# Block-sparse attention and a mixture of experts: weight splits with further buffers and in V's memory, transfers behind k's transposition, and score matmuls over 128 partitions

## The chip, the cores and the metric

The kernel runs on one core of one Trainium2 chip. The metric is the time of one execution on the device in microseconds (us); the kernel before takes 2201.07 us, the median of three runs (2196.04 to 2204.06). Its profile shows one further execution. The engines are called as the profile calls them: PE (TensorE, matmuls), PEld (PE's weight loads), DVE (VectorE), ACT (ScalarE), POOL (GpSimd) and SP (SyncE, which here issues all DMAs).

## The reference

Attention with a block mask comes first. Its output is the input x of a layer with eight experts, all of which are computed for every row and weighted by a matrix P that alternating row and column normalisation makes from x's logits.

```python
scores = 1.0 / np.sqrt(D) * np.matmul(q, k.transpose(0, 1, 3, 2))   # B, H, S, D = 4, 8, 768, 64
scores = np.where(mask, scores, -1e9)      # blocks of 32: window, first, last, 3 random ones
attn = softmax(scores)
x = (attn @ v).transpose(0, 2, 1, 3).reshape(B * S, H * D)          # 3072 x 512
logits = x @ w_gate
P = np.exp(logits - logits.max())
for _ in range(8):
    P /= P.sum(1, keepdims=True) + 1e-09
    P /= P.sum(0, keepdims=True) + 1e-09
    P *= N / E
for e in range(8):
    out += P[:, e:e + 1] * (np.maximum(x @ w1[e], 0.0) @ w2[e])      # 512 -> 1024 -> 512
```

## The kernel before

**Numbers as pairs.** Inputs are float32, matmuls take float16. A float32 operand is therefore split into a high and a low float16 part, and a product is three matmuls into one accumulator: high by high, high by low, low by high. A weight quadrant is split by an ACT instruction for the high part (`first_high` L275, `queue_split` L1184) and one or two DVE instructions for the low part (`first_low` L278, L1191).

**Attention.** 32 pairs of batch and head ("heads", n = 0 to 31) of six column tiles each make 192 steps T. A step has score matmuls twice: `m` (L689, L692), whose row maximum DVE takes (`top`, L698), and `t` (L722, L725), with the maximum subtracted through extra rows, whose exponential ACT takes (`pe`, L730). The first matmul of each covers 128 rows; the second one adds the low part of q and the masks' rows and covers only the rows in use, `ROWS_M` = 88 or `ROWS_T` = 98 (L443). `split_lo` (L740 to L744) finishes the weights, `values` (L787) multiplies by V three steps later, and L806 to L825 normalise and write x. Heads are handled two at a time, so a pair has 12 steps. `turn` (L675) turns q (16 steps ahead) and k (14 steps ahead, phase 4 of 6) by DMA; the scores of the pair begin 10 steps ahead of its weights. `lower` (L702) fills in rows that belong to the maxima and turns q's second part again (L710).

**The order.** A planner fixes the place of every instruction in attention. Fixed pieces stand at a step and a class (`at`); chains of optional jobs (weight loads, their sums, their splits) are dealt into steps by `deal()`, from planned microseconds of DVE, ACT and POOL for each. Each engine then runs its instructions in that order. SP runs in order too, and waits with an instruction until its source is ready.

**The passage from one to the other.** As soon as a batch's x is there, `x_split` and `x_store` (L303 to L313) split its column blocks for the expert layer and store them (384 KB each) in `xd`; `load_x1` (L247) loads the first tiles back. Expert 0's `w1` is loaded, scaled by its maximum, summed and split during attention. Its `w2` is loaded and scaled there and has four of its eight sums made; all of its seven splits come after attention. Of batch 3, the last steps of x (`finish_x` L373) run `LATE` = 34 product slots into the expert layer.

**The expert layer.** A stage i = 4e + b is expert e on batch b. Both matrix products go by a scheme of seven products on quadrants. `stage1` (L1315) has four column parts qi; in each the products p = 0, 1, 5, 6, 3, 4, 2 come as six groups of three matmuls of 128x384, land in four PSUM banks, and are combined by DVE (`comb`, L1336), ACT (L1371) and POOL; a column part takes about 13.8 us. `stage2` (L1435) makes the products `py` in the order 1, 0, 5, 6, 3, 4, 2 and adds them into `acc` (L1464 to L1480). One expert takes about 221 us. Products of stage i + 1 alternate with outputs of stage i. Beside them a queue of side work (`Slots`, L1109) runs weight splits when the planned time of the engine allows it, or when a product needs them (`need`).

**The weights of the next expert.** `w1` has one set of seven float16 buffers (`w1p`, in the arena and the attic, L236 to L245). In the last column part of an expert's last batch, each product p, once issued, frees its buffer, and `split_w1` (L1216) queues the split of the next expert's quadrant into it (L1324, `used[p]()`). All seven splits thus lie between the first products of that column part and the first ones of the next expert. `w2` has seven buffers of 4 KB (`w2p`, L1076), refilled during the next expert's stages by `split_w2` (L1239).

## Time and profile before

| quantity | value |
|---|---|
| median of three runs | 2201.07 us |
| profiled execution | 2201.64 us |
| its span | 2199.9 us, 1.74 us less than its time |
| PE, share of the span busy | 98% |
| DVE | 78% |
| POOL | 65% |
| ACT | 58% |
| attention | the first 415 us |
| one expert | about 221 us |
| granted TensorE clock, mean | 0.998 |

A group row of the profile names line, engine, operation, output and inputs, shape and count, then the busy time in us with the mean of one instruction in ns, and after a second bar the time for which the engine stood idle just before such instructions, with what ended that time. A timeline row has the start and the duration in us, then the same names, and in brackets the idle time before it. A window row has its bounds, its length, and for each engine the busy time and the number of instructions in it; at its end the granted clock, the share of the DMA engines and their GB/s.

### The profile page before, as it was taken

To read this page: it belongs to the slowest core of one execution; us is meant where nothing else is said; L and a number is where in the kernel's file an instruction comes from. 1 tells how busy PE (TensorE), PEld (TensorE's weight loads), DVE (VectorE), ACT (ScalarE), POOL (GpSimd) and SP (SyncE) were. 2 spreads that over 40 slices of the span, in tenths; PEclk is the share of its full clock that TensorE was granted. 3 is DMA by queue.
4 is the path that set the end of the run, shared out by engine and by line. 5 is a ranking of instruction groups with operands and counts; after the bars stand their busy time and mean duration, and the time that the engine had idled before them with its cause. 6 is when DMAs were issued, how large, how long until landed. Compare 5 with 4: busy or idle time off the path is not lost.

```text
span 2199.9 us, 47055 instructions
## 1 busy us (share of the span) xinstructions
PE 2150.8 (98%) x18796; PEld 1591.8 (72%) x18796; DVE 1706.8 (78%) x2970; ACT 1282.8 (58%) x2385; POOL 1432.6 (65%) x1476
## 2 busy tenths in 40 slices
PE   6999999999999999999999999999999999999999
PEld 4777676667777777777777777777777777777777
DVE  8889889677878767876887688768876887688765
ACT  5888888666466546554655465546554655465442
POOL 4667768477568656765676567656765686567553
PEclk9999999999999999999999999999999999999999
DMA  6757796122121212121212121212121212131221
GB/s 170 180 130 171 171 198 146 42 100 84 58 89 51 90 51 90 51 90 51 89 52 89 51 89 51 89 51 89 51 89 51 90 51 89 51 90 58 80 80 51
DMA packets 195632, 192.34 MB, mean 87 GB/s; under 512 B 132412, under 2 KB 150868, under 8 KB 195412
## 3 DMA queue, kind: packets, MB, share of 16 engines
q1 hardware_dynamic: 194848, 189.30, 30.6%
q8 instruction: 147, 2.41, 0.4%
q14 instruction: 73, 0.60, 0.1%
q10 hardware_dynamic: 564, 0.03, 0.0%
HBM read 140.54 MB, written 17.30 MB: 72 GB/s over the span
## 4 chain that ended last, share of the span: by engine, by line
PE 72%; DVE 11%; POOL 7%; ACT 4%; issue 4%; DMA 1%; POOLq 0%; DVEq 0%; ACTq 0%
PE py L1456 31%; PE p L1324 30%; PE u L787 3%; PE m L689 2%; PE t L722 2%; PE m L692 2%; PE t L725 2%; POOL h L1356 2%; DVE top L698 1%; ACT h L1345 1%; POOL s L1404 1%; DMA kt<-ks 1%; POOL r L1202 1%; DVE h L1356 1%; DVE attic L1191 1%
## 5 line engine op out<-in xcount | busy, mean ns | idle before, releaser
L1456 PE MATMUL py<-w2p,h 128*128 128x256 f16 x8064 | 973.2, 273 | 6.3 <-DVE acc L1480 2.6
L1456 PEld LDWEIGHTS <-h 128*128 128x128 f16 x8064 | 788.9, 98 | 159.0 <-issue 7.4
L1356 POOL TENSOR_TENSOR h<-u,h 128x384 f16<-128x384 f32 x128 | 126.4, 988 | 534.8 <-ACT h L1345 534.8
L1324 PE MATMUL p<-attic 128*128 128x384 f16 x2304 | 421.4, 326 | 3.9 <-DVE attic L1191 2.1
L1324 PEld LDWEIGHTS <-attic 128*128 128x128 f16 x3072 | 299.2, 98 | 173.1 <-DVE attic L1191 6.6
L1324 PE MATMUL p<-arena 128*128 128x384 f16 x2304 | 417.1, 326 | 4.2 <-DVE arena L1191 1.7
L1480 DVE SCALAR_TENSOR_TENSOR acc<-py,spare,acc 128x256 f32<-128x256 f32 (+1 forms) x588 | 299.8, 514 | 90.9 <-PE py L1456 85.5
L1345 ACT ACTIVATE h<-c 128x384 f16<-128x384 f32 x256 | 132.5, 518 | 348.3 <-DVE c L1336 301.2
L1324 PEld LDWEIGHTS <-arena 128*128 128x128 f16 x2304 | 224.9, 98 | 128.4 <-issue 3.5
L1336 DVE SCALAR_TENSOR_TENSOR a<-p,a 128x384 f32<-128x384 f32 x384 | 211.4, 550 | 20.8 <-PE p L1324 9.0
L1356 DVE TENSOR_TENSOR h<-s,h 128x384 f16<-128x384 f32 x128 | 113.2, 884 | 146.6 <-ACT h L1345 146.5
L698 DVE TENSOR_REDUCE top<-m 128x1 f32<-128x768 f32 x192 | 181.8, 951 | 41.0 <-PE m L692 40.3
L730 ACT ACTIVATE pe<-t,qk 128x768 int32<-128x768 f32 x192 | 172.3, 899 | 69.8 <-PE t L725 58.7
L1209 POOL TENSOR_TENSOR c<-c,r 128x384 f32<-128x384 f32 x128 | 159.1, 1243 | 10.0
L1345 ACT ACTIVATE h<-r 128x384 f16<-128x384 f32 x256 | 129.8, 516 | 60.4 <-POOL r L1209 58.8
L1209 POOL TENSOR_TENSOR r<-s,r 128x384 f32<-128x384 f32 x128 | 157.9, 1234 | 10.0
L744 POOL TENSOR_SCALAR pl<-pe 128x768 f16<-128x768 uint16 x125 | 108.9, 874 | 72.2 <-ACT pe L730 69.7
L1404 POOL TENSOR_TENSOR s<-a,u 128x384 f32<-128x384 f32 x128 | 133.0, 1039 | 30.9 <-ACT a L1401 30.1
L1356 POOL TENSOR_TENSOR h<-r,h 128x384 f16<-128x384 f32 x128 | 146.0, 1140 | 6.0 <-ACT h L1345 6.0
L1324 PE MATMUL p<-arena,attic 128*128 128x384 f16 x768 | 145.9, 326 | 0.0
L787 PE MATMUL u<-vq,pl 128*128 128x65 f16 x1152 | 142.2, 193 | 0.3 <-ACT pl L742 0.3
L689 PE MATMUL m<-kt,qt 128*128 128x512 f16 (+1 forms) x384 | 127.7, 333 | 15.2 <-DMA kt<-ks 10.9
(196 smaller groups left out, 3704.1 us busy)
## 6 DMA issues: line engine op xcount, KB each, us to landing
arena<-xd SPq DMA_DIRECT2D x128, 384.0 KB, 3.4
attic<-xd SPq DMA_DIRECT2D x96, 384.0 KB, 3.6
r<-in_moe_w_dram SPq DMA_DIRECT2D x14, 2048.0 KB, 8.6
arena<-in_q_dram SPq DMA_DIRECT2D x16, 384.0 KB, 4.2
arena<-in_k_dram SPq DMA_DIRECT2D x16, 384.0 KB, 4.6
vraw<-in_v_dram SPq DMA_DIRECT2D x16, 384.0 KB, 5.6
xd<-xs_t SPq DMA_DIRECT2D x16, 384.0 KB, 4.3
out_dram<-acc SPq DMA_DIRECT2D x48, 128.0 KB, 1.7
```

Source lines behind the costliest of these rows:

```text
L689: nc.tensor.matmul(sc[:, lo:hi], lhsT=qt[:, 0, c], rhs=ka[:, lo:hi], start=True, stop=False)
L698: nc.vector.tensor_reduce(out=tops[n][:, c : c + 1], in_=sc[:, :S], axis=AX.X, op=ALU.max)
L730: nc.scalar.activation(pe, sc[:, :S], AF.Exp, bias=EXP_SHIFT, scale=qk[n // 2][3])
L787: nc.tensor.matmul(uv[:, c, :n], lhsT=l[:, c * P : (c + 1) * P], rhs=w[:, h, kc, :n], start=(kc == 0 and c == 0 and m == 0), stop=(kc == N ...
L1209: nc.gpsimd.tensor_tensor(out=out, in0=x, in1=y, op=ALU.subtract)
L1324: nc.tensor.matmul(ps, lhsT=w1p[p][:, l, kc, fs], rhs=xp[p][:, r, kc], start=(kc == 0 and m == 0), stop=(kc == KH - 1 and m == 2),)
L1336: nc.vector.scalar_tensor_tensor(out=t, in0=ps, scalar=HDOWN, in1=other, op0=ALU.mult, op1=ALU.add)
L1345: nc.scalar.activation(h[:, 0], src, AF.Relu if relu else AF.Copy)
L1356: eng.tensor_tensor(out=h[:, 1], in0=src, in1=h[:, 0], op=ALU.subtract)
L1404: nc.gpsimd.tensor_tensor(out=s1, in0=a1, in1=u3, op=ALU.add)
L1456: nc.tensor.matmul(py, lhsT=hs[i, p, kc][:, l, tsl], rhs=w2p[p][:, r, kc], start=(old is None and kc == 0 and m == 0), stop=(kc == KF // 2 ...
L1480: nc.vector.scalar_tensor_tensor(out=dst, in0=src, scalar=c, in1=dst, op0=ALU.mult, op1=ALU.add)
```

## The change

Six edits are made together.

1. **Transfers behind k's transposition.** `calm_step` moves a step of phase 1, 2 or 3 of six to phase 4, the phase of k's transposition; it is applied to the stores of x and the loads of the first x tiles. The quarters of a weight load may be issued in phases 0, 4, 5, 6, 10 and 11 of twelve only, one step apart instead of three.
2. **The second score matmuls** cover 128 partitions. So that the added rows are zero where it matters, POOL clears two columns of `qs` (128x6x2) for each of 29 heads.
3. **`w2` of expert 0.** V's raw input lies in a `vault` that stays; three `w2p` buffers (p = 1, 0, 5) are laid into it, since V is no longer read by then. All eight sums and three splits of `w2` (high by ACT, low by DVE in two halves) are planned at attention's end, whose planner now runs 12 steps longer. In the expert layer p = 6, 4, 3, 2 are left.
4. **`w1` of the next experts.** Three spare buffers of 4 KB let `split_w1(e + 1)` be queued in stage b = 1, behind its sums, for p = 0, 1 and 6, with both sums. The other four (5, 3, 4, 2) follow into the old buffers of 0, 1, 5 and 6 in the last column part; the old buffers of 3, 4 and 2 become the next spares.
5. **The spread of the scale** (a small matmul) may also come in phase 7 for `w2`.
6. **`LATE`** is 22 instead of 34.

```diff
-LATE = 34
+LATE = 22
+ROOM = 12
...
+    w2p = {
+        p: carve(4 * KB * n, F16, 2, KF // 2, DH, home=vault)
+        for n, p in enumerate((1, 0, 5))
+    }
...
+    def calm_step(T):
+        return T + (4 - T) % NC if 0 < T % NC < 4 else T
...
-                    at(T + 3, LAST, x_store, b, f"b{j}{k}", p)
+                    at(calm_step(T + 3), LAST, x_store, b, f"b{j}{k}", p)
...
-        ROWS_M, ROWS_T = D + NB, D + 34
+        ROWS_M = ROWS_T = P
...
-        vraw = vsp.tile([P, H, NC, D], F32, name="vraw")
+        vraw = vault.rearrange("p (h c d) -> p h c d", h=H, c=NC)
...
             src, s, hi, _ = parts_qk(n, m)
+            if m == 0 and n >= NQS:
+                nc.gpsimd.memset(qss[n % NQS][:, 1, :, AT_M : AT_M + 2], 0.0)
...
+        CALM = (0, 4, 5, 6, 10, 11)
...
                     job((nm, "load", n), lambda n=n: load_part(which, 0, n, 4),
-                        after=((((nm, "load", n - 1), 3),) if n else ()))
+                        after=((((nm, "load", n - 1), 1),) if n else ()), phase=CALM)
...
         for p, T in zip(PORDER, (164, 166, 175, 177, 120, 124, 128)):
-            at(T, LAST, load_x1, 0, p)
+            at(calm_step(T), LAST, load_x1, 0, p)
...
-        for T in range(min(plan_at), max(plan_at) + 1):
+        for T in range(min(plan_at), max(plan_at) + ROOM):
...
     def split_w1(e):
         a, s3 = wr["a"], wr["s3"]
+        old = w1ps[e - 1]
+        new = w1ps[e] = {p: spares.pop(0) for p in (0, 1, 6)}
...
+        one(0, a[0, 0])
+        queue_sum(a[0, 0], a[1, 0], a[0, 0], ("w1", e, 5))
+        one(1, a[0, 1])
+        queue_sum(a[0, 1], a[0, 1], a[0, 0], ("w1", e, 2))
+        one(6, s3)
+        spares.extend(old[p] for p in (3, 4, 2))
...
+        return dict((
+            follow(5, a[0, 0], 0), follow(3, a[1, 1], 1),
+            follow(4, a[1, 0], 5), follow(2, a[0, 1], 6),
+        ))
...
-            yield from stage1(i, qi, split_w1(e + 1) if swap else None)
+            yield from stage1(i, qi, follows[e + 1] if swap else None)
...
             sum_w1(e + 1)
+            follows[e + 1] = split_w1(e + 1)
```

What stands on SP around the transposition of k for the last head, first before the change; `qt` and `kt` are the turned q and k, `qs` and `ks` their sources, `xd` the stored x, `arena` the first x tiles of the expert layer:

```order
L710 DMA_TRANSPOSE qt_103<-qs_112 128x6x128
L677 DMA_TRANSPOSE qt_105<-qs_111 128x12x128
L313 DMA xd_79<-xs_t_7119 128x1536
L677 DMA_TRANSPOSE kt_109<-ks_114 128x12x128
L313 DMA xd_79<-xs_t_7274 128x1536
L247 DMA arena<-xd_77 128x1536
```

The same place after the change:

```order
L257 DMA arena<-xd_77 128x1536 x2
L727 DMA_TRANSPOSE qt_107<-qs_116 128x6x128
L694 DMA_TRANSPOSE qt_109<-qs_115 128x12x128
L694 DMA_TRANSPOSE kt_113<-ks_118 128x12x128
L325 DMA xd_79<-xs_t_7151 128x1536
L325 DMA xd_79<-xs_t_7305 128x1536
```

The store that stood between the two transpositions of L677 now stands behind k's.

What stands on ACT at attention's end, before the change; `pe` are the exponentials of the last four column tiles, `xf` the last transposed x, `a` and `r` the first combinations of stage 0:

```order
L730 ACTIVATE pe_3_7873<-t_3_7868,qk_15_6550 128x768
L825 ACTIVATE xf_6862<-u_148 128x384
L730 ACTIVATE pe_4_7904<-t_4_7899,qk_15_6550 128x768
L730 ACTIVATE pe_5_7931<-t_5_7926,qk_15_6550 128x768
L1371 ACTIVATE a_0_0_8081<-p_0_0_8082 128x384
L1376 ACTIVATE r_0_0_8092<-r_0_0_8092 128x384
```

The same place after the change; L286 are the high parts of `w2`, `vault` their buffers:

```order
L747 ACTIVATE pe_3_7905<-t_3_7900,qk_15_6578 128x768
L286 ACTIVATE vault<-r_0_5756,sw_0_5759 128x1024
L842 ACTIVATE xf_6893<-u_151 128x384
L747 ACTIVATE pe_4_7937<-t_4_7932,qk_15_6578 128x768
L286 ACTIVATE vault<-r_0_5756,sw_0_5759 128x1024
L747 ACTIVATE pe_5_7967<-t_5_7962,qk_15_6578 128x768
L759 ACTIVATE pl_5_7969<-pe_5_7967 128x768
L1426 ACTIVATE a_0_0_8126<-p_0_0_8127 128x384
L286 ACTIVATE vault<-r_0_5756,sw_0_5759 128x1024
L1431 ACTIVATE r_0_0_8135<-r_0_0_8135 128x384
```

Three high parts (p = 1, 0, 5) have come among the last exponentials, and the last `pl` has gone from DVE to ACT.

What stands on DVE at the same place after the change; `u`, `c` and `h` belong to the first column part of stage 0, L823 to L825 to the last head's normalisation:

```order
L757 TENSOR_SCALAR pl_3_7907<-pe_3_7905 128x768
L291 SCALAR_TENSOR_TENSOR vault<-r_0_5756,sw_0_5759,vault 128x512 x4
L1391 SCALAR_TENSOR_TENSOR r_0_0_8135<-p_0_0_8136,a_0_0_8126 128x384
L1391 SCALAR_TENSOR_TENSOR a_0_0_8126<-p_0_0_8147,a_0_0_8126 128x384
L1391 SCALAR_TENSOR_TENSOR u_0_0_8155<-p_0_0_8156,a_0_0_8126 128x384
L823 TENSOR_SCALAR r_8040<-u_152 128x6
L1411 TENSOR_TENSOR h_8091<-r_0_0_8135,h_8091 128x384
L824 RECIPROCAL r_8040<-r_8040 128x6
L825 TENSOR_TENSOR xn_3_7885<-u_152,r_8040 128x6x64
L291 SCALAR_TENSOR_TENSOR vault<-r_0_5756,sw_0_5759,vault 128x512 x2
L1391 SCALAR_TENSOR_TENSOR c_0_0_8164<-p_0_0_8165,u_0_0_8155 128x384
```

None of the six L291 rows stood there before; the last two of them now stand between `xn` and the combination `c_0_0`.

What stands on DVE where expert 4 begins (stage 16), before the change; `attic<-r` are low parts of the new `w1`, `py` and `acc` the outputs of stage 15:

```order
L1356 TENSOR_TENSOR h_8074<-a_15_3_18274,h_8074 128x384
L1191 SCALAR_TENSOR_TENSOR attic<-r_4_17148,sw_4_17152,attic 128x1024
L1336 SCALAR_TENSOR_TENSOR r_16_0_18505<-p_16_0_18506,a_16_0_18496 128x384
L1480 SCALAR_TENSOR_TENSOR acc_9853<-py_0_0_18516,spare_16462,acc_9853 128x256
L1356 TENSOR_TENSOR h_8050<-r_16_0_18505,h_8050 128x384
L1336 SCALAR_TENSOR_TENSOR a_16_0_18496<-p_16_0_18531,a_16_0_18496 128x384
L1191 SCALAR_TENSOR_TENSOR attic<-r_4_17148,sw_4_17152,attic 128x1024
L1336 SCALAR_TENSOR_TENSOR u_16_0_18541<-p_16_0_18542,a_16_0_18496 128x384
L1480 SCALAR_TENSOR_TENSOR acc_9853<-py_0_1_18550,spare_16462,acc_9853 128x256
L1191 SCALAR_TENSOR_TENSOR attic<-r_4_17148,sw_4_17152,attic 128x1024
L1336 SCALAR_TENSOR_TENSOR c_16_0_18565<-p_16_0_18566,u_16_0_18541 128x384
```

The same place after the change:

```order
L1535 SCALAR_TENSOR_TENSOR acc_9893<-py_4_2_18368,spare_16493,acc_9893 128x256
L1237 SCALAR_TENSOR_TENSOR attic<-r_4_17179,sw_4_17183,attic 128x1024
L1535 SCALAR_TENSOR_TENSOR acc_9894<-py_1_0_18481,spare_16493,acc_9894 128x256
L1411 TENSOR_TENSOR h_8115<-s_15_3_18452,h_8115 128x384
L1535 SCALAR_TENSOR_TENSOR acc_9894<-py_1_1_18496,spare_16493,acc_9894 128x256
L1411 TENSOR_TENSOR h_8116<-a_15_3_18315,h_8116 128x384
L1535 SCALAR_TENSOR_TENSOR acc_9894<-py_1_2_18513,spare_16493,acc_9894 128x256
L1391 SCALAR_TENSOR_TENSOR r_16_0_18539<-p_16_0_18540,a_16_0_18530 128x384
L1535 SCALAR_TENSOR_TENSOR acc_9894<-py_0_0_18551,spare_16493,acc_9894 128x256
L1411 TENSOR_TENSOR h_8092<-r_16_0_18539,h_8092 128x384
L1391 SCALAR_TENSOR_TENSOR a_16_0_18530<-p_16_0_18565,a_16_0_18530 128x384
L1391 SCALAR_TENSOR_TENSOR u_16_0_18573<-p_16_0_18574,a_16_0_18530 128x384
```

The three low parts that stood among the first combinations of stage 16 are gone from there; the last of the seven now stands ahead of them, and three stand in stage 14.

More of the change, by code (lines that the diff above doesn't have):

```diff
@@ L370, in plan_x @@
             at(T, LATER, x_split, b, nm, o)
[L371 removed]
+            at(calm_step(T + 3), LAST, x_store, b, nm, p)
     def finish_x(b):
@@ L950, in sum_chain @@
                 job((nm, "sum", k), lambda k=k: run_sum(k), (0.0, 0.0, 1.45), after=marks(k))
-                for k in range(8 if which == 1 else 4)
+                for k in range(8)
             ))
@@ L1074, in tile_sparse_attention_moe @@
     ps_y = mpool("ps_y", 4, space=PSUM)
-    w2p = [big.tile([P, 2, KF // 2, DH], F16, name=f"w2p_{p}") for p in range(NP)]
+    for p in (6, 4, 3, 2):
+        w2p[p] = big.tile([P, 2, KF // 2, DH], F16, name=f"w2p_{p}")
     hfree = [
@@ L1080, in tile_sparse_attention_moe @@
     accs = {b: big.tile([P, NC, DM], F32, name=f"acc_{b}") for b in range(B // 2)}
+    w1ps = {0: w1p}
+    spares = [big.tile([P, 2, KH, FH], F16, name=f"w1p_{n}") for n in range(3)]
+    follows = {}
     bank[0] = lambda nm: ps_h.tile([P, 512], F32, tag="ph", name=nm)
@@ L1263, in split_w2 @@
             first,
-            lambda: (one(6, m[0, 1]), one(5, m[0, 0])),
+            second,
             lambda: (one(4, t1), one(3, m[1, 0]), one(2, m[1, 1])),
```

90 lines of the change are left out of this document (57 added, 33 removed).

## The prediction

> **What bounds the kernel now.** I read the page's shares first, then windows, to see where PE is not full, then PE's waits, and last the single places on the timeline.
>
> ```profile
> span 2199.9 us, 47055 instructions
> PE 2150.8 (98%) x18796; PEld 1591.8 (72%) x18796; DVE 1706.8 (78%) x2970; ACT 1282.8 (58%) x2385; POOL 1432.6 (65%) x1476
> ```
>
> PE is busy for 2150.8 of 2199.9 us. Idle is 2199.9 − 2150.8 = 49.1 us, and no edit here takes a matmul away: the whole change can win at most what of these 49.1 us it reaches.
>
> ```profile
> 0.00:20.00 20.00, 5.20 (x23) 2.74 (x24) 14.43 (x37) 8.67 (x15) 8.65 (x29) 1.00 0.92 263
> 20.00:40.00 20.00, 17.32 (x108) 9.03 (x107) 17.48 (x36) 9.02 (x13) 8.49 (x15) 0.83 0.49 91
> 1000.00:1200.00 200.00, 199.19 (x1528) 149.00 (x1527) 154.68 (x265) 108.65 (x218) 130.09 (x123) 1.00 0.25 76
> ```
>
> The first 40 us hold 40 − 5.20 − 17.32 = 17.5 us of the idle time; nothing of the change is placed there. At most 49.1 − 17.5 = 31.6 us are left. In the steady expert layer PE is busy for 199.19 of 200 us, so what can be won lies at single places, which PE's waits name (engine, line waited for: us in total, times, longest):
>
> ```profile
> PE m L689 <- DMA kt<-ks: 10.9, 4, 6.3
> PE py L1456 <- DVE acc L1480: 2.6, 7, 0.9
> PE p L1324 <- DVE attic L1191: 2.1, 5, 0.4
> PE py L1456 <- ACT w2p L1187: 2.1, 1, 2.1
> PE p L1324 <- DVE arena L1191: 1.7, 1, 1.7
> PE p L1324 <- ACT a L1371: 1.1, 2, 0.6
> PE py L1456 <- ACT acc L1477: 0.7, 1, 0.7
> ```
>
> Each of these names an edit: k's transposition, the splits of `w1` (L1191 into attic and arena), the splits of `w2` (L1187), and the combinations that stand behind splits (L1371, L1477).
>
> **k's transposition.** Of the four waits the one of 6.3 us is the first head's, which stays. The other three:
>
> ```profile
> 80.62 0.38 PE L689 MATMUL m<-kt,qt 128*128 128x512 f16 x1 [0.51 <-DMA kt<-ks]
> 321.57 0.38 PE L689 MATMUL m<-kt,qt 128*128 128x512 f16 x1 [1.38 <-DMA kt<-ks]
> 388.21 0.38 PE L689 MATMUL m<-kt,qt 128*128 128x512 f16 x1 [2.73 <-DMA kt<-ks]
> ```
>
> They sum to 0.51 + 1.38 + 2.73 = 4.62 us. On SP's timeline the last two have another transfer ahead of k's:
>
> ```profile
> 313.49 0.57 SPq L191 DMA_DIRECT2D r<-in_moe_w_dram  x1
> 314.15 1.46 SPq L677 DMA_TRANSPOSE kt<-ks  x1
> ...
> 381.74 0.54 SPq L313 DMA_DIRECT2D xd<-xs_t  x1
> 382.37 1.48 SPq L677 DMA_TRANSPOSE kt<-ks  x1
> ```
>
> The order puts both behind k's transposition. k's then starts earlier by the issue (0.6 us) and by the data ahead of it in the queue. I take −4.4, nearly all, bounded by 0 and −4.6. At the first place two loads of V stay ahead of k's, so a part of its 0.51 may remain. What is late next is DVE's `top`: in the stretch behind the second place DVE is nearly full.
>
> ```profile
> 340.00:360.00 20.00, 19.06 (x294) 13.86 (x290) 19.72 (x29) 16.55 (x23) 18.43 (x23) 1.00 0.72 174
> ```
>
> DVE runs 19.72 of 20 us there, so what PE wins 20 us earlier DVE may take back; that is the upper bound, 0. The moved loads now stand three in a row ahead of `lower`'s transposition of q (L710), which is needed only four steps of 1.96 us later, so nothing waits for it.
>
> **128 rows and the cleared columns.** The second matmuls against the first, which already cover 128 rows:
>
> ```profile
> L689 PE MATMUL m<-kt,qt 128*128 128x512 f16 x192 | 74.3, 387 | 15.2 <-DMA kt<-ks 10.9 <-DVE top L698 2.3 <-ACT pe L730 1.8
> L692 PE MATMUL m<-kt,qt 88*128 88x512 f16 x192 | 74.9, 390 | 0.0
> L722 PE MATMUL t<-qt,kt 128*128 128x512 f16 x192 | 73.2, 381 | 4.3 <-DVE top L698 3.5 <-DVE qk L647 0.2
> L725 PE MATMUL t<-qt,kt 98*128 98x512 f16 x192 | 73.5, 383 | 0.0
> ```
>
> 88 rows take 390 ns against 387, 98 rows 383 against 381: 192 × (3 + 2) ns = 1.0 us. I take −1.0, bounded by 0 and −1.0. More rows are thus not dearer. The Trainium skill ("TensorE: Matmul & The Clock Gate", section "🎯 Why this matters for your kernels") says that one matmul of few rows takes as long as one of 128; by it the term would be 0 and the sum 1.0 us higher, while the rows here lean 2 to 3 ns the other way.
>
> Clearing 128x6x2 on POOL 29 times has no row; the nearest are a 128x6 addition and a clearing of 128x12:
>
> ```profile
> L709 POOL TENSOR_TENSOR qs<-low,qs 128x6 f16<-128x6 f32 x32 | 7.4, 231 | 2.8
> L493 POOL MEMSET ks<- 128x12 f16 x2 | 0.5, 481 | 0.0
> ```
>
> At 0.23 to 0.48 us each that is 7 to 14 us of POOL, one per six steps. POOL's free time covers it: even in the full stretch from 340 us it has 20 − 18.43 = 1.57 us free for its one or two clearings. I take 0, bounded by 0 and +1, since there DVE and PE lean on POOL's results.
>
> **`w2` split at attention's end.** Today all seven splits lie in stage 0, and PE waits for them once at 463.57 us (the 2.1 of the waits) and 12 us later behind an ACT queue full of them (the 0.7). With three splits and four sums gone from there I take −3.0: 2.1 + 0.7, and 0.2 of small waits between. The bounds are 0 and −4.7, the latter with all of the early `acc` waits as well.
>
> Against it stands the place that they move to. These rows set the pace there:
>
> ```profile
> L276 ACT ACTIVATE attic<-r,sw 128x1024 f16<-128x1024 f32 x3 | 3.4, 1138 | 0.0
> L279 DVE SCALAR_TENSOR_TENSOR attic<-r,sw,attic 128x512 f16<-128x512 f32 x6 | 6.3, 1042 | 0.0
> L934 POOL TENSOR_TENSOR t<-r 128x512 f32<-128x512 f32 x2 | 2.5, 1270 | 0.1
> ...
> 410.13 0.90 ACT L730 ACTIVATE pe<-t,qk 128x768 int32<-128x768 f32 x1 [0.30 <-PE t L725]
> 410.93 0.48 ACT L825 ACTIVATE xf<-u 128x384 f32<-128x384 f32 x1
> ...
> 419.91 0.55 DVE L1336 SCALAR_TENSOR_TENSOR c<-p,u 128x384 f32<-128x384 f32 x1
> ...
> 422.77 2.11 PE L1324 MATMUL p<-arena 128*128 128x384 f16 x12
> ```
>
> In the new order the chain is this. `pe_3` ends at 410.13 + 0.90 = 411.0. High 1 (1.14), `xf` (0.48), `pe_4` (0.90) and high 0 (1.14) follow on ACT: 414.7. DVE makes low 0 in two halves, 2 × 1.04: 416.8. The two sums that overwrite its source take 2 × 1.27 on POOL: 419.3. High 5 on ACT takes 1.14: 420.5. Between it and low 5 stand `r` and `h` on ACT (0.5 each), and on DVE `h` and `xn` (0.56 each): about 422.7. Low 5 takes 2 × 1.04: about 424.8, and only then comes the combination `c_0_0` (0.55): about 425.4, where it was done at 420.5 before. `c_0_0` empties the bank of the fifth product, which the ninth needs: the group that started at 422.77. PE would wait some 2.6 us; I take +2.5, bounded by 0 (low 5 finds the same wait that DVE had anyway) and +4. So this edit is worth −0.5.
>
> DVE's split may also be slowed by POOL's sums beside it; the rows of `h` (L1356) show the size of that, 0.56 us alone and 1.35 under a POOL instruction:
>
> ```profile
> 418.02 0.56 DVE L1356 TENSOR_TENSOR h<-r,h 128x384 f16<-128x384 f32 x1 [0.23 <-ACT h L1345]
> ...
> 427.14 1.35 DVE L1356 TENSOR_TENSOR h<-a,h 128x384 f16<-128x384 f32 x1
> ```
>
> That is in the +4. The Trainium skill ("SBUF — State Buffer", section "Who interferes with whom") gives the reason: VectorE's second port pair is GpSimd's, and one locks the other out for an instruction. By it low 5 beside one more sum of 1.27 us would come 1.3 later and the sum would be 1.3 us higher; the two rows agree with it.
>
> **`w1` with spares.** Seven switches of expert. Waits of matmuls for splits are 2.1 + 1.7 = 3.8 us; those of the weight loads ahead of them, which come first in the pipe, are larger (the attic's row here, arena's being one wait of 2.0):
>
> ```profile
> L1324 PEld LDWEIGHTS <-attic 128*128 128x128 f16 x3072 | 299.2, 98 | 173.1 <-DVE attic L1191 6.6 <-issue 2.7
> L1324 PEld LDWEIGHTS <-arena 128*128 128x128 f16 x2304 | 224.9, 98 | 128.4 <-issue 3.5 <-DVE arena L1191 2.0
> ```
>
> 6.6 + 2.0 = 8.6 us. The matmul's idle time understates a loss, since its modelled end reaches past the next start; the weight load's overstates it, as a load may be late without cost. I take −6.0, near the middle, bounded by −3.8 and −8.6. In the new order all low parts stand ahead of the new expert's combinations, so these waits can go whole.
>
> Three splits and two sums now lie in stages b = 2 instead. Their DVE parts are the rows of L1191:
>
> ```profile
> L1191 DVE SCALAR_TENSOR_TENSOR arena<-r,sw,arena 128x1024 f16<-128x1024 f32 x21 | 34.6, 1650 | 0.0
> ```
>
> 3 × 1.65 = 5.0 us of DVE, let in when its planned time allows. In the steady window DVE has 200 − 154.68 = 45 us of 200 free. `w2`'s seven splits, let in the same way, cost the `acc` waits of 2.6 us in all, over seven experts 0.37 each; three of seven would be 0.16, times 7 = +1.1. The bounds are 0 and +2.6. With the last splits out of the way, the combinations that start a new expert (L1371, 1.1 us of waits) come in time: −1.0, bounded by 0 and −1.1.
>
> **`LATE`, the sums' phases, the spread.** The 12 slots shift the last steps of x, with their costs, to other places of stages 0 and 1. Whether they meet a gap or a full stretch I can't read from before: 0, bounded by ±2.4, the 1.1 that PE waits now for the logits in that stretch (494.19 us on its timeline) and half of the acc waits around it.
>
> ```profile
> 494.19 0.18 PE L332 MATMUL lg<-gate,xs_b 128*128 128x8 f16 x1 [1.15 <-DVE xs_b L391]
> ```
>
> **The sum.** −4.4 − 1.0 + 0 − 3.0 + 2.5 − 6.0 + 1.1 − 1.0 + 0 = −11.8 us. The profiled execution took 2201.64 (its span and 1.74 around it), so 2189.8; it stands 0.57 above the median, so 2189.3, and I say **2189**. About 0.5% (11 us, that is 2190.1 and 2212.1) is what a measurement of this kernel can tell from no change, and the forecast lies on that line.
>
> **Rivals.** *All of it works, and the tail is clean.* The +2.5 does not come, because low 5 falls into time that DVE idles, and the `w1` waits go in full (−8.6): −11.8 − 2.5 − 2.6 = −16.9, and with the bank waits the small ones go too, about 2183. For it: in the last window of attention DVE and POOL have time.
>
> ```profile
> 400.00:420.00 20.00, 19.68 (x311) 14.74 (x308) 10.73 (x31) 12.53 (x17) 1.26 (x3) 1.00 0.05 11
> ```
>
> DVE is busy 10.73 of 20 us and POOL 1.26. Against it: the chain above is a chain of dependent steps over three engines, which free time doesn't shorten.
>
> *The freed time is taken back.* k's −4.4 is lost to the full DVE behind it, the `w1` waits shrink by 3.8 only, and the tail costs 4: −11.8 + 4.4 + 2.2 + 1.5 = −3.7, and half of the stage 0 gain gone, about −5.5: 2196. For it speak the 19.72 us above; against it that PE's waits for k's are long, single ones.
>
> *Slower: early `w1` splits overfill DVE.* Five us of splits in a column part of 13.8 us. DVE runs at 154.68/200 = 77% on average with its splits, so a column part has 0.23 × 13.8 = 3.2 us free. If all three came in one, and that already held a `w2` split, nothing would be hidden: 7 × 5.0 = 35 us, less the 11.8: about 2224. It decides from the point at which DVE's work in a column part passes 13.8 us; until then it costs nothing. Against it stand the rule that lets a split in only if planned time allows, and `w2`'s splits, which cost 0.37 per expert.
>
> **How the numbers follow.** Forecast, 2184 to 2194: 0.50, of which 0.29 lie below 2190.1. Clean tail, 2183: 0.22, all faster. Taken back, 2196: 0.22, all within 0.5%. Overfilled DVE, 2224: 0.06. So faster 0.51, same 0.43, slower 0.06. The range leaves out the slower case and the outer halves of the two others' spread (about 0.06 on each side): 2178 to 2200.
>
> **What would show it.** Right: the two later waits of `m` for `kt` are gone, and those of `p` for L1191's successors; the wait of `py` for `w2p` at 463 us too; and a new wait of 2 to 3 us stands near 423 us, for the combination behind low 5. The second score matmuls last as long as the first. Wrong: idle time of `m` for `top` grows after 320 us by what k's gave; or new waits for `acc` and `a` in stages b = 2 sum to over 3 us; or PE's busy time itself changes by more than a few us, which none of my terms holds but the 128 rows.

## The result, and the profile after

| | before | changed |
|---|---|---|
| median | 2197.98 us (6 runs, 2194.85 to 2204.06) | 2179.49 us (6 runs, 2177.34 to 2181.36) |
| ratio | | 0.9915, 95% interval 0.9903 to 0.9926 |
| once more, beside other kernels (e5) | 2201.61 us | 2179.34 us, ratio 0.9905 (0.9893 to 0.9917) |

The change makes the kernel 18.5 to 22.3 us faster (2197.98 − 2179.49; 2201.61 − 2179.34). The forecast was 2189 us, some 12 us faster: the direction was right and the size too small. The page of the changed kernel, its first two lines:

```profile
span 2179.5 us, 47067 instructions
PE 2142.1 (98%) x18796; PEld 1592.0 (73%) x18796; DVE 1694.2 (78%) x2971; ACT 1284.3 (59%) x2387; POOL 1441.2 (66%) x1501
```

PE has the same 18796 matmuls, but is busy for 8.7 us less (2150.8 − 2142.1), and idle for 37.4 instead of 49.1 us. Nearly all of the forecast was of the second kind; a change of PE's busy time by more than a few us was among the prediction's own signs of being wrong. PE's waits in the changed kernel:

```profile
PE m L706 <- DMA kt<-ks: 8.5, 3, 6.5
...
PE all_lg L119 <- DVE spare L1330: 1.6, 1, 1.6
PE cs L1348 <- DVE spare L1342: 1.5, 1, 1.5
...
PE py L1511 <- ACT acc L1532: 0.4, 1, 0.4
PE py L1511 <- DVE acc L1535: 0.4, 2, 0.2
...
PE p L1379 <- DVE c L1391: 0.2, 1, 0.2
```

Of the lines that the prediction started from, those for splits (attic, arena, `w2p`) are gone altogether, and `acc` is down from 2.6 to 0.4. The two later waits for k's transposition (1.38 and 2.73 us before) are gone as foretold. Its line still has two besides the first head's: 0.65 us at 78.66 us, where the prediction let a part stay, and 1.38 at 173.40, where there was none before. A second profile of the same program has neither (e5 below). New are the two for `all_lg` and `cs`, matmuls of the normalisation of P, which `LATE` = 22 moved forward. The predicted wait of 2 to 3 us behind attention's end is not there: the 0.2 us for `c` in the list stand at 433.87 us, one column part later.

In three stretches, windows show where PE's time changed (columns as before; the last three are the granted clock, the DMA share and GB/s). First the kernel before, then the changed one:

```profile
26.00:40.00 14.00, 11.98 (x83) 6.47 (x83) 11.69 (x21) 6.43 (x9) 7.21 (x11) 0.76 0.64 111
600.00:640.00 40.00, 37.48 (x287) 27.56 (x285) 35.20 (x59) 22.70 (x41) 25.79 (x21) 1.00 0.23 70
640.00:700.00 60.00, 58.02 (x438) 42.51 (x437) 43.99 (x83) 39.15 (x83) 46.74 (x47) 1.00 0.27 82
```

```profile
26.00:40.00 14.00, 10.77 (x109) 6.88 (x109) 13.49 (x26) 7.14 (x10) 8.71 (x16) 1.00 0.62 126
600.00:640.00 40.00, 40.00 (x308) 29.86 (x306) 30.47 (x51) 25.23 (x53) 22.08 (x20) 1.00 0.38 123
640.00:700.00 60.00, 59.94 (x460) 44.67 (x459) 46.46 (x84) 39.07 (x77) 47.99 (x47) 1.00 0.15 47
```

From 26 to 40 us PE starts 109 matmuls instead of 83 at a granted clock of 1.00 instead of 0.76: a gain in a place where the prediction put none. From 600 to 700 us PE has gone from 4.50 us idle to 0.06: this is the first switch of expert and what surrounds it.

Setting both traces side by side by the number of matmuls started gives the course: the changed kernel leads by 2.0 us at the 400th matmul (59 us), 4.4 at the 4800th (383), 7.4 at the 5200th (412), 10.7 at the 6000th (516), then only 6.9 at the 6400th (570), 12.5 at the 7600th (733) and 20.4 at the last.

### The profile page after: what moved, and what is told of

It reads as the page before. It is cut to its first block, busy times and chain, and to the rows that moved or that the text cites. A ratio compares the mean times of both kernels' runs of the same rounds, so it can differ in the third digit from the quotient of the medians.

```text
span 2179.5 us, 47067 instructions
## 1 busy us (share of the span) xinstructions
PE 2142.1 (98%) x18796; PEld 1592.0 (73%) x18796; DVE 1694.2 (78%) x2971; ACT 1284.3 (59%) x2387; POOL 1441.2 (66%) x1501
## 4 chain that ended last, share of the span: by engine, by line
PE 86%; DVE 6%; POOL 3%; ACT 2%; issue 2%; DMA 1%; DVEq 0%; POOLq 0%; ACTq 0%
PE py L1511 38%; PE p L1379 37%; PE u L804 3%; PE t L739 2%; PE t L742 2%; PE m L706 2%; PE m L709 2%; DVE top L715 1%; DMA kt<-ks 1%; POOL h L1411 1%; DVE h L1411 1%; ACT pe L747 1%; ACT h L1400 1%; DVE vl L615 0%; POOL s L1459 0%
## 5 line engine op out<-in xcount | busy, mean ns | idle before, releaser
L1511 PE MATMUL py<-w2p,h 128*128 128x256 f16 x4608 | 564.8, 273 | 0.7 <-ACT acc L1532 0.4
L1411 POOL TENSOR_TENSOR h<-u,h 128x384 f16<-128x384 f32 x128 | 132.0, 1031 | 516.9 <-ACT h L1400 516.9
L1511 PE MATMUL py<-vault,h 128*128 128x256 f16 x3456 | 413.3, 273 | 0.8 <-DVE h L1405 0.5
L1379 PEld LDWEIGHTS <-attic 128*128 128x128 f16 x2208 | 216.5, 98 | 121.5 <-issue 2.4
L1379 PEld LDWEIGHTS <-arena 128*128 128x128 f16 x1728 | 168.7, 98 | 91.9 <-issue 1.2
L1379 PE MATMUL p<-attic 128*128 128x384 f16 x1152 | 213.7, 328 | 0.0
L1379 PE MATMUL p<-arena 128*128 128x384 f16 x1152 | 210.9, 326 | 0.4 <-DVE c L1391 0.2
L1379 PEld LDWEIGHTS <-w1p 128*128 128x128 f16 x1440 | 140.7, 98 | 77.7 <-issue 0.6
L1379 PE MATMUL p<-arena,attic 128*128 128x384 f16 x1056 | 194.8, 326 | 0.0
L1379 PE MATMUL p<-arena,w1p 128*128 128x384 f16 x864 | 161.3, 326 | 0.0
```

The costliest lines, as they stand in the source:

```text
L1379: nc.tensor.matmul(ps, lhsT=w1ps[i // B][p][:, l, kc, fs], rhs=xp[p][:, r, kc], start=(kc == 0 and m == 0), stop=(kc == KH - 1 and m == 2),)
L1411: eng.tensor_tensor(out=h[:, 1], in0=src, in1=h[:, 0], op=ALU.subtract)
L1511: nc.tensor.matmul(py, lhsT=hs[i, p, kc][:, l, tsl], rhs=w2p[p][:, r, kc], start=(old is None and kc == 0 and m == 0), stop=(kc == KF // 2 ...
```

## The experiments

Each removal is the changed kernel with one part undone, each addition the kernel before with one part alone. All do the whole computation. The gain or loss in us is a difference of medians against the changed kernel (2179.4) for removals, and the ratio times the median of the kernel before in the same session for additions. A ratio's interval is about ±0.0012, or ±2.6 us. The changed kernel itself ran in two sessions only, first with the kernel before and then (e5) beside e6, e7 and e8; the median of the kernel before moved between 2197.7 and 2201.6 us from session to session. So a difference of under some 3 us is not clear by its time, and stands here only as far as the traces bear it out. The `w2` splits were not run alone in the kernel before, and the fifth edit, the spread, was not tried apart.

| run | what | median, us | ratio (interval) |
|---|---|---|---|
| e1 | 88 and 98 rows back | 2183.76 | 0.9931 (0.9919 to 0.9944) |
| e2 | no `w1` spares | 2187.38 | 0.9946 (0.9934 to 0.9958) |
| e3 | `w2` splits in the expert layer | 2186.02 | 0.9938 (0.9925 to 0.9952) |
| e4 | `LATE` = 34 | 2183.14 | 0.9927 (0.9915 to 0.9940) |
| e5 | changed, again | 2179.34 | 0.9905 (0.9893 to 0.9917) |
| e6 | transfers at their old places | 2180.90 | 0.9912 (0.9899 to 0.9926) |
| e7 | `LATE` = 28 | 2185.12 | 0.9930 (0.9918 to 0.9942) |
| e8 | before, `LATE` = 22 | 2201.68 | 1.0002 (0.9992 to 1.0013) |
| e9 | before, 128 rows | 2192.41 | 0.9974 (0.9964 to 0.9984) |
| e10 | before, transfers moved | 2192.37 | 0.9982 (0.9974 to 0.9990) |
| e11 | split of the first normalisation step | 2182.29 | 0.9933 (0.9920 to 0.9945) |
| e12 | e11 and a longer gap | 2181.04 | 0.9926 (0.9914 to 0.9939) |
| e13 | before, `w1` spares | 2194.77 | 0.9981 (0.9968 to 0.9995) |
| e14 | before, 128 rows and transfers | 2191.29 | 0.9967 (0.9957 to 0.9976) |
| e15 | e3 with `LATE` = 34 | 2186.58 | 0.9951 (0.9936 to 0.9966) |
| e16 | `LATE` = 19 | 2182.16 | 0.9929 (0.9915 to 0.9943) |
| e17 | e11, one slot only | 2181.34 | 0.9919 (0.9903 to 0.9935) |
| e18 | e17 with `LATE` = 21 | 2179.94 | 0.9914 (0.9897 to 0.9930) |

### Rows: e1 and e9

```diff
-        ROWS_M = ROWS_T = P
+        ROWS_M, ROWS_T = D + NB, D + 34
...
-            if m == 0 and n >= NQS:
-                nc.gpsimd.memset(qss[n % NQS][:, 1, :, AT_M : AT_M + 2], 0.0)
```

> The changed kernel with the second score matmuls over 88 and 98 rows again and without the cleared columns. The prediction's term says that this is 1.0 us slower than the changed kernel (192 times 3 + 2 ns). Rival, from the two traces: in a stretch of attention in which PE waits for nothing the changed kernel gains 0.28 to 0.29 us in 400 matmuls (11 us of it from 87 to 145 us), which over attention's 5200 matmuls is some 3.5 us. The first gives a ratio to the kernel before of 0.9915 + 0.0005 = 0.992, the second 0.993; the profile decides better than the ratio: the same stretch must lose 0.28 us per 400 matmuls by the rival and 0.07 by the prediction's term.

e9 makes the opposite edit on the kernel before.

> The kernel before with the second score matmuls over 128 rows and the cleared columns, nothing else. The granted clock fell to half for some 6 us near 28 to 35 us in the profiles of the kernel before, of e1 and of e8, which all have 88 and 98 rows, and in none of the seven others, which have 128. If the rows cause it, this kernel's clock stays at 1.00 from 26 to 40 us, which is worth 1.8 us, and with some 2 us over the rest of attention it is 3.9 us faster than the kernel before: ratio 0.998. By the prediction's term, 1.0 us: 0.9995, and the clock falls as before.

e1 is 4.3 us slower than the changed kernel (2183.76 − 2179.4), e9 is 5.7 us faster than the one before (0.0026 × 2197.71). Both speak for the larger value. The window from 26 to 40 us, first of e1 and then of e9, holds the part that comes from the clock:

```profile
26.00:40.00 14.00, 11.72 (x83) 6.33 (x83) 11.48 (x18) 6.29 (x9) 6.94 (x11) 0.76 0.65 116
```

```profile
26.00:40.00 14.00, 11.00 (x110) 6.99 (x110) 13.53 (x25) 7.27 (x10) 8.73 (x16) 1.00 0.71 128
```

Only the rows (and their clearing) differ between e1 and the changed kernel, and between e9 and the one before, and the clock goes with them in both directions. So it is in every profile taken: 0.76, 0.76, 0.76, 0.88 and 0.76 in the five kernels with 88 and 98 rows (before, e1, e8, e10, e13), 1.00 in the fifteen others. The lead at the 400th matmul over the kernel before, 2.0 us in the changed kernel and 2.2 in e9, is nearly all this. The mean clocks of all executions agree. In e9's session the kernel before had a mean granted clock of 0.997 or 0.998 in 16 of 21 executions (median 2198.8 us) and of 0.999 or 1.000 in the other five (2194.5 us): the fall comes in most of its executions, not in all. All 21 executions of e9 and e14, which add the 128 rows, had 0.999 or 1.000. At an equal clock e9 (2192.4 us) is then some 2 us faster than the kernel before, and the other 3 to 4 us go with the clock.

The rest is in the starts of the matmuls. A full stretch of 50 us, of the kernel before and of e9:

```profile
95.00:145.00 50.00, 50.00 (x694) 36.08 (x691) 41.45 (x79) 38.53 (x53) 31.13 (x46) 1.00 0.57 125
```

```profile
95.00:145.00 50.00, 50.00 (x702) 36.24 (x699) 41.62 (x80) 39.12 (x55) 30.51 (x51) 1.00 0.59 128
```

PE waits for nothing in either, and starts 702 matmuls instead of 694, 1.1% more. From start to start in the traces of e1 and of the changed kernel, a matmul behind a 512-wide one of 88 or 98 rows comes after 220 ns instead of 216, behind a 256-wide one after 112 instead of 109, and a 256-wide matmul of 128 rows followed by one of fewer also takes 112 instead of 109: 4 + 3 + 3 = 10 ns, twice in each of 192 steps, is 3.8 us if nothing else holds PE. Not all of it is seen: between the 400th and the 5200th matmul e1 wins 7.0 us on the kernel before. The changed kernel wins 8.9 in e5's profile, 1.9 more, and 5.4 in its first profile, which with that profile's two waits for k left out (2.0 us, e5 below) is 0.5 more. That the rest is taken back where DVE is full was not shown.

### Transfers behind k's transposition: e6, e10 and e14

```diff
-        return T + (4 - T) % NC if 0 < T % NC < 4 else T
+        return T
...
-                        after=((((nm, "load", n - 1), 1),) if n else ()), phase=CALM)
+                        after=((((nm, "load", n - 1), 3),) if n else ()))
```

> The changed kernel with the stores of x, the loads of the first x tiles and the weight loads back at their old phases. By the prediction's term 4.4 us slower than the changed kernel (ratio 0.9935), with waits of m for kt near 314 and 381 us back, 1.4 and 2.7 us. Rival (time won is taken back by the full DVE): under 2 us slower, since the win at the second place did not show in the trace of the changed kernel until some steps later; ratio 0.992, with more idle time for top in the profile of the changed kernel than in this one.

e10 makes the change's edit alone on the kernel before, e14 with the 128 rows added.

> The kernel before with the stores and loads behind k's transposition, nothing else. By the prediction's term 4.4 us faster, 0.998. From e6, where their return cost 1.5 us though the waits of 0.9 and 2.7 us for k came back: what is won before attention's end is given back in the first stage, where the order of DVE, ACT and POOL and not PE sets the pace. If that holds without the w2 splits in attention as well, this is 1.5 to 2.5 us faster, 0.999. If it is those splits that take it back, the full 4.4.

> The kernel before with 128 rows and with the transfers behind k's transposition. If the two are independent, 5.7 + 4.0 = 9.7 us faster, 0.9956. If they share a wait, as e6 and e9 suggest (e9 lost the wait for k near 388 us without moving any transfer), 6.5 to 7.5 us faster, 0.9968.

e6 is 1.5 us slower than the changed kernel (2180.90 − 2179.4), e10 4.0 us faster than the one before (0.0018 × 2197.71), e14 7.3 (0.0033 × 2199.54). The waits behave as foretold: in e10 and e14 only the first head's is left, in e6 three others are back:

```profile
PE m L692 <- DMA kt<-ks: 6.3, 1, 6.3
```

```profile
PE m L706 <- DMA kt<-ks: 9.0, 4, 6.2
```

The first line is e10's, the second e6's. But the time depends on what is there besides. With the 128 rows, the same edit adds 7.3 − 5.7 = 1.6 us, not 4.0, though the intervals of the two sessions leave room for either. One reason is in the traces: e9, which moves no transfer, has waits of only 1.16 and 1.21 us for k, where the kernel before had 0.51, 1.38 and 2.73. Nor need all of e10's 4.0 us be k's: its profile leads the kernel before by 1.8 us at the 400th matmul already, with the shorter fall of the clock (0.88), and only 5 of its 12 executions had a mean clock of 0.998, the rest more. The gain was not lost to `top`, as a rival had it: PE's waits for it are 6.5 us in e5 and 6.2 in e6. In the traces of the changed kernel and of e6, the 2.9 us that e6 falls behind between the 4800th and the 5200th matmul shrink by 1.8 over the next 400, in the expert layer's first stage. That the first stage swallows part of a gain is seen there; which engine does it was not settled.

### What differs by chance: e5

> The changed kernel once more, unaltered, beside the others. If the ratio of 0.9915 holds, it is 0.991 to 0.993 here. What is asked of its profile: whether three things that differ between the profile of the changed kernel and those of e1 to e4, in stretches in which their programs are the same, come and go by chance. These are the half clock for some 4 us behind a stall (522 to 527 us, lost 2.6 us), waits for k's transposition of 0.8 and 1.5 us at 77 and 172 us, and waits of outputs for acc of 0.5 us in six of seven experts, which the changed kernel's profile lacks and e1, e3 and e4 show. If these are chance, at least one of the three differs in this profile from the first one. If they belong to the program, all three are as in the first profile.

The ratio holds within its interval. The profile of the same program has one wait for k instead of three, and the waits for `acc` that the first profile lacked (1.1 us instead of 0.4): these two come and go without a change of program. The half clock does not tell the two profiles apart; it lasts about 3.4 us in both, behind the wait for `all_lg`. But in the profiles of e2 and e6, which have the same wait of 1.6 us, the clock stays at 1.00. For the waits for `acc` the traces show what decides. POOL's four sums behind a split meet one DVE instruction; first the changed kernel, then e1, each with DVE's row and POOL's:

```profile
899.14 0.56 DVE L1405 SCALAR_TENSOR_TENSOR h<-c,h 128x384 f16<-128x384 f32 x1 [0.59 <-ACT h L1400]
...
897.80 4.25 POOL L1248 TENSOR_TENSOR r<-r 128x256 f32<-128x256 f32 x4
```

```profile
899.69 1.16 DVE L1403 SCALAR_TENSOR_TENSOR h<-c,h 128x384 f16<-128x384 f32 x1 [0.59 <-ACT h L1398]
...
898.34 3.11 POOL L1246 TENSOR_TENSOR r<-r 128x256 f32<-128x256 f32 x4
```

Up to there DVE and POOL run the same rows with the same durations in both. In the one, POOL waits (4.25 against 3.11) and DVE runs at once; in the other, DVE waits (1.16 against 0.56), its outputs come later, and PE loses some 0.5 us a little later, once in each expert in which it falls so. This agrees with the Trainium skill ("SBUF — State Buffer", section "Who interferes with whom"), by which the two engines share a pair of ports that one holds for an instruction at a time. Up to 3 us of the 20.4 between the two first profiles are such luck; the two waits for k, 2.0 us, went the other way.

### `w1` spares: e2 and e13

```diff
-        old = w1ps[e - 1]
-        new = w1ps[e] = {p: spares.pop(0) for p in (0, 1, 6)}
...
-            follows[e + 1] = split_w1(e + 1)
...
-            yield from stage1(i, qi, follows[e + 1] if swap else None)
+            yield from stage1(i, qi, split_w1(e + 1) if swap else None)
```

> The changed kernel with expert weights w1 split as before, all seven in the last column part. By the prediction (w1 -6.0 + 1.1, start of an expert -1.0) 5.9 us slower than the changed kernel: ratio 0.994. Rival, from the two traces: behind the first 600 us the changed kernel gains 13.8 us on the one before (6.5 at 607 us, 20.4 at the end), more than any other edit can touch there; if all of that belongs to the spares this is 13 us slower, ratio 0.997 to 0.998. A third possibility: the small gains of 0.4 to 0.5 us in the stage behind an expert's first one (waits of outputs for acc) belong to another edit; then the switches alone come back, 0.9 us each for the later six and some 3 for the first, 8 to 9 us, ratio 0.9955.

e13 puts the spares alone into the kernel before.

> The kernel before with the w1 spares alone. By the prediction's terms (-6.0 + 1.1 - 1.0) 5.9 us faster, ratio 0.9973. By e2, where their removal cost 7.9 us in all, of which six switches of expert of 0.9 us each in its trace, 5.4 at least and up to 8 us faster: 0.9964 to 0.9975. If the spares need the w2 splits out of stage 0 to be worth anything at the first switch, the lower end.

e2 is 8.0 us slower than the changed kernel (2187.38 − 2179.4), e13 only 4.2 us faster than the one before (0.0019 × 2199.54, with an interval from 1 to 7). At each switch of expert but the first, both pairs of traces show the same 0.8 to 0.9 us, 5.3 in all six. They differ around the first switch. There e13 falls 6.1 us behind the kernel before between the 5200th and the 6800th matmul (412 to 622 us), of which it wins 3.8 back by the 7600th. Its trace has a wait there that the kernel before has not, and POOL's rows ahead of it name the new work:

```profile
560.34 3.49 POOL L1205 TENSOR_TENSOR r<-r 128x512 f32<-128x512 f32 x2
563.79 1.31 POOL L401 TENSOR_TENSOR xf<-xf 128x384 f32<-128x384 f32 x1
...
573.08 1.25 PE L1462 MATMUL py<-w2p,h 128*128 128x256 f16 x10 [2.50 <-ACT acc L1483]
```

L1205 are sums of the next `w1`, which the spares have moved from the end of the expert (616 us in the kernel before) into its third stage, b = 2; L401 is a late step of x. POOL gets to the combinations of the stage only after them, ACT (which copies `acc`) waits in order behind those, and PE for ACT: 2.5 us, with waits of 1.2 and 0.7 us ahead of it and three for `cs` (1.9 us in all).

### `w2` splits and `LATE`: e3, e4, e15, e7 and e8

```diff
-                for k in range(8)
+                for k in range(8 if which == 1 else 4)
...
-        chain(*splits)
...
         def sums():
+            one(1, m[1, 0])
             if e:
-                one(1, m[1, 0])
```

> The changed kernel with the four further sums and the three splits of the first w2 left to the expert layer, as before. By the prediction (-3.0 and +2.5) 0.5 us slower than the changed kernel, ratio 0.992. Rival, from the trace of the changed kernel, which shows no wait of 2 to 3 us at attention's end: only the gain is there, and this is 3 us slower or more, ratio 0.993; the wait of PE for the w2 split of about 2 us is then back near 450 to 465 us in its trace.

```diff
-LATE = 22
+LATE = 34
```

> The changed kernel with LATE = 34. The prediction's term is 0. Rival, from the trace of the changed kernel: PE waits 1.6 us for the normalisation's matmul all_lg at 521 us and 1.5 us for cs at 560 us, which the kernel before did not have in this size; with the clock at half speed behind the first of them that is about 4 us more than before. If LATE = 22 brought that, this kernel is 3 to 4 us faster than the changed one, ratio 0.990; if the other edits brought it, the time is the same or slower, 0.9915 and up.

> The changed kernel with the four sums and three splits of the first w2 left to the expert layer and with LATE = 34. If LATE = 22 is worth something only because the w2 splits are out of the way, as the equal waits of e3 and e4 and the unchanged time of e8 say, this is as slow as e3: 0.993 to 0.9945. If the two are independent, 0.9955.

> The changed kernel with LATE = 28, between the two values tried. With 22 PE waits for all_lg (1.6 us, and half clock behind it) and cs (1.5), with 34 for acc (2.5) and cs (1.9). If the steps of batch 3 only slide along, one of these waits goes and no other comes: 2 to 3 us faster than the changed kernel, ratio 0.990. If what counts is that they are done before the first w1 splits and outputs of stage 2 crowd in, 28 is between or as slow as 34: 0.992 to 0.993.

> The kernel before with LATE = 22 alone. The prediction's term is 0. From e3 and e4, whose traces show the same waits at 548 to 694 us though one has LATE = 22 and the other has the w2 splits out of the way, I now think that both are needed: with all seven w2 splits in stage 0 the late steps cannot run earlier. Then this is the same as the kernel before, 0.9995 to 1.0005. If LATE is worth its 3.4 us by itself, the ratio is 0.9985.

e3 is 6.6 us slower than the changed kernel, e4 3.7, and both edits together (e15) 7.2: they do not add. `LATE` = 28 is no middle way (5.7 slower), and `LATE` = 22 in the kernel before does nothing (ratio 1.0002). The reason stands in the traces of e3 and of e4:

```profile
560.13 1.52 PE L1482 MATMUL py<-vault,h 128*128 128x256 f16 x10 [2.50 <-ACT acc L1503]
```

```profile
558.22 1.25 PE L1511 MATMUL py<-vault,h 128*128 128x256 f16 x10 [2.49 <-ACT acc L1532]
```

It is e13's wait, with the same 2.5 us and the same smaller ones around it; e7 and e15 have it too. No other kernel here has it: neither those without spares nor those with spares, the early `w2` splits and `LATE` of 22 or less. What they differ in is where the late steps of x stand on POOL, first in e4, then in the changed kernel:

```profile
545.50 3.48 POOL L1248 TENSOR_TENSOR r<-r 128x512 f32<-128x512 f32 x2
548.95 1.32 POOL L416 TENSOR_TENSOR xf<-xf 128x384 f32<-128x384 f32 x1
```

```profile
503.96 4.18 POOL L416 TENSOR_TENSOR xf<-xf 128x384 f32<-128x384 f32 x4
```

In e4 the last of them stand right behind the early sums of `w1`, as in e13, e3, e7 and e15. In the changed kernel the last four end at 508 us, ahead of all these sums. So the spares bring a collision between the early `w1` work and the late steps of x, and it is avoided only if the late steps come before it. That needs a smaller `LATE`, and it needs engines that are not still splitting `w2`: with `LATE` = 22 but all `w2` splits in the first stages (e3, and e8 without spares) the late steps run at 500 to 554 and 510 to 546 us, as late as with 34. The rival written down for e4, that `LATE` = 22 had cost 4 us, was wrong: it bought these waits off at the price of the two of the normalisation (1.6 and 1.5 us). In the traces the collision costs 3.1 to 3.7 us between the 6000th and the 7600th matmul (e4 and e3 against e5). Of e3's 6.6 us, 2.1 are the old wait for the `w2` split in the first stage, which is back:

```profile
PE py L1482 <- ACT vault L1210: 2.1, 1, 2.1
```

### A better version was not found: e16, e11, e12, e17 and e18

The changed kernel's largest wait left in the expert layer is the one for `all_lg`, with a spell of half clock behind it:

```profile
522.56 0.32 PE L119 MATMUL all_lg<-ident,spare 128*128 128x128 f32 x1 [1.61 <-DVE spare L1330]
...
524.00:526.00 2.00, 2.00 (x8) 0.95 (x7) 0.56 (x1) 1.12 (x2) 2.00 (x2) 0.50 0.00 0
```

Five kernels tried to place it elsewhere. e16 has `LATE` = 19. The others have the step in two:

```diff
             nc.vector.tensor_reduce(out=m, in_=flat(lg), axis=AX.X, op=ALU.max)
+
+        def weigh_all():
             nc.vector.tensor_reduce(out=m, in_=spread_max(m, "lg"), axis=AX.X, op=ALU.max)
...
-        slots.add(weigh, ("balance",), 1, True, dve=0.5)
+        slots.add(weigh, ("balance",), 1, True, dve=0.3)
+        slots.add(weigh_all, ("balance",), 2, True, dve=0.5, gap=3)
```

> The changed kernel with LATE = 19. The normalisation comes three slots earlier. If its waits (1.6 us for all_lg, 1.5 for cs) are matters of place, one of them goes, 1.5 to 3 us faster than the changed kernel, 0.9895 to 0.990. If the late steps are held by the planned time of the engines and not by LATE, the same, 0.991.

> The changed kernel with the first step of the normalisation in two: DVE's maximum in one slot, PE's transposition of it (all_lg) with the rest three slots later. If PE's wait of 1.6 us for all_lg and the half clock that follows it in some executions come from that order alone, 1.8 to 3 us faster than the changed kernel, ratio 0.990. If the wait only moves to the next matmul of the normalisation (cs), the same as the changed kernel.

> As e11, and each cs matmul of the normalisation four slots behind DVE's part of it instead of three. If the wait of 1.5 us for cs is such an order too, another 1.5 us faster: ratio 0.989. If the longer normalisation meets the later splits, as with LATE = 28 and 34, slower again, 0.992.

> The changed kernel with the first step of the normalisation in two, PE's all_lg one slot behind DVE's maximum. If the wait of 1.6 us for all_lg is a matter of one slot and the rest moves only 2 us, 1.8 to 3 us faster than the changed kernel, 0.990. If every shift of the normalisation meets the splits of the next w1, as with LATE = 28 and e11, 1.5 to 3 us slower, 0.992 to 0.9925.

> As e17 with LATE = 21, so that everything behind all_lg stands where it stands in the changed kernel. If the wait can be bought out by one slot, 1.8 to 3 us faster than the changed kernel, 0.990. If the late steps, one slot earlier, wait for the logits as with LATE = 19 (1.1 us there), the same, 0.991.

None is faster: e16 is 2.7 us slower and e11 2.9; the 1.6 of e12, 1.9 of e17 and 0.5 of e18 are within the noise. In e11 the wait for `all_lg` is gone, and those for `cs` have grown to more than both were:

```profile
PE cs L1350 <- DVE spare L1344: 6.8, 4, 2.4
```

With one slot (e17, e18) the 1.6 us for `all_lg` stayed as they were, since DVE itself comes to its maximum late (at 519.09 us in e17, `all_lg` right behind it at 519.49), and those for `cs` rose to 4.2 and 4.6. In these traces the wait goes with DVE's fill at that place and moves with the normalisation. No kernel that was run is faster than the changed one.

## Why the forecast was too small

The step that failed is the sum itself, which took the edits as independent, and in it two terms: `w2`'s splits with `LATE`, put at −3.0 + 2.5 and 0 and worth 7.2 us together, and the 128 rows, put at −1.0 and worth 4.3 to 5.7. Three kernels build the change up. Rows and transfers alone bring 7.3 us (e14), where the sum had 5.4. With the spares, but without `w2`'s splits and `LATE` = 22, it is 10.8 (e15: 0.0049 × 2199.54), where the sum had 11.3: that this comes out is luck, rows too small against transfers and spares too large. The last pair takes it to 18.5 to 20.9, where the sum had 11.8.

- **`w2`'s splits and `LATE`.** The −3.0 held: between the 5200th and the 6000th matmul, in the first stage, the changed kernel wins 3.3 us on the one before (7.4 to 10.7), and 2.2 on e3. The +2.5 did not come. The chain has the shape that was written down, and each of its rows is in the changed kernel's trace, ACT's, DVE's, and PE's at the bank:

```profile
402.69 0.90 ACT L747 ACTIVATE pe<-t,qk 128x768 int32<-128x768 f32 x1 [0.28 <-PE t L742]
...
410.68 1.15 ACT L286 ACTIVATE vault<-r,sw 128x1024 f16<-128x1024 f32 x1 [1.64 <-POOL r L952]
...
414.14 1.41 DVE L291 SCALAR_TENSOR_TENSOR vault<-r,sw,vault 128x512 f16<-128x512 f32 x2
415.47 0.55 DVE L1391 SCALAR_TENSOR_TENSOR c<-p,u 128x384 f32<-128x384 f32 x1
...
416.07 2.27 PE L1379 MATMUL p<-arena 128*128 128x384 f16 x12
```

  From the end of `pe_3` (403.6) to that of `c` (416.0) it takes 12.4 us, where 14.4 were worked out (411.0 to 425.4). Two halves of a low part took 1.41 us and not 2.08; the 1.04 was a mean over halves most of which ran beside POOL. And PE came for the bank 12.5 us after `pe_3`, not 11.8 (422.8 − 411.0), and 0.51 of this is a wait for a `pl` on POOL at 406.83. So `c` was done just before PE came, and nothing was left to wait. With 0.05 us between the two, it is luck that no wait came of it.
- **`LATE`** was put at 0 with ±2.4, as an edit by itself, and by itself it is 0 (e8). What the prediction did not see is that the spares need it: e13 gives back 6.1 us in the stages around 550 to 620 us, of which it wins 3.8 again. The first stage's splits and `LATE` buy the collision off, 3.1 to 3.7 us, and each of them only with the other; this is why e3 and e4 cost more than their own waits. The new stalls of early splits were looked for in the stage's DVE; the collision was on POOL, through the sums that move with the splits.
- **The 128 rows** were put at −1.0 and brought 4.3 to 5.7 us. The step that failed is "88 rows take 390 ns against 387, 98 rows 383 against 381: 192 × (3 + 2) ns". It took the duration of the 512-wide matmuls for their cost, left out the 256-wide ones, and did not look at the distance to the next start. The sign that was named, second matmuls as long as the first, came true (384 against 385 ns, 379 against 378) and says nothing of that cost. "Nothing of the change is placed there", said of the first 40 us, was wrong, since the clock there follows the rows. The starts give 3.8 us at most, the clock 2 to 4. The sentence of the Trainium skill that few rows take as long as 128 ("TensorE: Matmul & The Clock Gate", section "🎯 Why this matters for your kernels") gives 0 for the term, which is further off than mine.
- **k's transposition** was put at −4.4: the waits that it named are gone, and by itself the edit brings 4.0 us (e10), part of which may be the clock's. Beside the rest of the change it is worth 1.5, which is no more than the noise. The 128 rows alone leave only 2.4 us of waits for k (e9).
- **The `w1` spares** were put at −5.9 in all. Six switches of 0.9 us, and the waits for splits gone from the list: the mechanism held, and its size within the noise, 4.2 alone (the collision taken off) and 8.0 on removal.
- **The rivals.** The clean tail came nearest, and its two signs came true: no wait for low 5, and the waits for `w1`'s splits gone in full. But its 2183 had neither the rows nor the collision in it. "Taken back" did not come: time was taken back in one place (the first stage, behind k's gain) and not by `top`. Its sum is also wrong as it stands: −3.7 with half of the first stage's gain lost is −2.2, so 2199 and not 2196. DVE overfilled by early splits in every expert did not come either: PE's waits for `acc` fell.

## What to carry to other kernels

Cost a matmul by the distance to the next start, over every width, and not by its own duration; and read the granted clock by windows, since an edit of shape can move it. Work that is moved out of one wait takes its sums and transfers along: look for what stands in the new place on every engine, above all where another queue of late work passes. Edits made together need a run of each alone and one with each left out, since `LATE` was worth nothing alone and 3.7 us beside the spares and the early splits.

## What the runs showed of the hardware

- The granted clock near 30 us was 0.57 over 8 us with second matmuls of 88 and 98 rows and 1.00 with 128, with PE busy for 7.38 and 6.36 of these 8 us:

```profile
28.00:36.00 8.00, 7.38 (x27) 3.28 (x26) 6.26 (x9) 4.38 (x6) 2.91 (x6) 0.57 0.50 101
```

```profile
28.00:36.00 8.00, 6.36 (x55) 3.78 (x54) 7.71 (x11) 5.26 (x8) 3.47 (x8) 1.00 0.57 113
```

  The first is the kernel before, the second e9. The Trainium skill ("TensorE: Matmul & The Clock Gate", section "🔬 Part 1: The HAM clock gate (the "warmup" mystery)") tells of a gate that watches how busy PE is; that rows count for it, it does not say. PE's busy time ahead of the fall does not tell the kernels apart: from 21 to 28 us it is 4.94 us in the kernel before and 4.59 in e9, and 3.98 in e1, where the clock falls, against 3.90 in e6, where it does not. By which mechanism the rows count was not shown here. That the clearing on POOL plays no part was not tried apart.
- A wait of PE of 1.6 us, for `all_lg`, was followed by about 3.4 us at a granted clock of 0.50 in the profiles of the changed kernel, e5 and e1, and by none in those of e2 and e6.
- Next to a matmul of another number of rows the next start came 3 to 4 ns later: 112 instead of 109 ns at a width of 256, 220 instead of 216 behind a 512-wide one of fewer rows. Behind a 512-wide one of 128 rows it made no difference (215 to 216).
- Clearing 128x6x2 on POOL took 0.11 us, half of the prediction's lower bound of 0.23 (the row is the changed kernel's):

```profile
L682 POOL MEMSET qs<- 128x12 f16 x29 | 3.2, 109 | 1.5 <-DMA qt<-qs 1.3
```
